# Block-causal attention and FFN: unscaled query split with its subtraction on POOL, single casts, last blocks by DMA, one PSUM bank less per pair

## The chip, the cores and the metric

The kernel runs on one core of a Trainium2 chip. Its engines are TensorE (PE; its weight loads are listed as PEld), VectorE (DVE), ScalarE (ACT), GpSimd (POOL) and SyncE (SP, which only issues DMAs here). Each engine executes its own instructions in order. The metric is the device time of one execution in microseconds, the median over runs.

## The reference

```python
# q, k, v: (8, 8, 576, 64) float32, block = 64
scores = q @ k.T / sqrt(64)
scores = where(row // block >= column // block, scores, -1e9)
attn = exp(scores - max(scores)); attn = attn / (sum(attn) + 1e-9)
x = (attn @ v).transpose(0, 2, 1, 3).reshape(4608, 512)
# w_in (512, 2048), w_out (2048, 512)
h = x @ w_in
g = where(h >= 1, h, where(h <= -1, 0, (h + 1) ** 2 / 4))
out = g @ w_out                      # (4608, 512)
```

## The kernel before

**Numbers.** Matmuls take float32r operands. A float32 value is kept as a sum of two float32r parts, hi (the value cast) and lo (the value less hi), and a product of two such values is made of several matmuls. Queries, keys, values, weights and the FFN's activations are all split so. Attention weights are split too, from the third batch on (the first two are PLAIN and keep theirs in float32).

**Attention** goes over 32 pairs (8 batches by 4 pairs of heads). Each pair is 8 steps of the generator `attention_steps`, whose text sets the order; a scheduler then orders each engine's instructions, and each engine keeps to that order. The names:

- `load` brings q, k and v of the next pair into a pool of three buffers (qn, kn, vn; `nat`). vn takes the buffer that qn had, and it is free once the q subtraction has read it.
- `split_q` and `split_k` make hi and lo side by side (qs, ks), 9 pieces of 64 columns each: 4 tiles for each of two heads and one piece of last blocks. q is multiplied by SCALE = 1/8 in this place. The lo part of q is made on VectorE (L311), that of k on POOL (L321).
- `turned` transposes four 128x128 tiles on TensorE into a bank (ps_qk), ScalarE copies the bank to qb or kb, and SyncE copies half the rows on to qa or ka by DMA. `turned_last` does it with the last block (64 rows) of both heads; there VectorE makes the second copy (L371).
- `scores(j, g)` makes the scores of head j for the query tiles of group g (0, 1, 2), with maxima (L414), exponentials (L418, with the sums), the reciprocal of sum + EPS (L400, L401) and the scaling (L424). `scores_last` does the last 64 query rows of both heads in two halves of 288 columns (L438 to L450).
- The scaled weights pr go through a SyncE DMA into a float32r tile, prr (L246), so that TensorE can transpose them at its float32r rate.
- `turn(j, g)` transposes prr into a bank (ps_t) and `split` makes hi on ScalarE (L454) and lo on VectorE (L456): pa, pb. `turn_last` does this for the last rows; the last key block goes to the tiles pcs (pc), in a bank of its own.
- `attn_v(j)` and `attn_v_first` multiply with the split values (vsr); the last two matmuls of `attn_v` read pcs.

**FFN** is 9 chunks of 512 tokens by 16 columns of w_in. `ffn_in` is 12 matmuls into ph, then the activation (L655 to L661: ACT, DVE, DVE, ACT, POOL); `ffn_out` is 12 matmuls into four output banks. From step 36 of attention on, each step is followed by one FFN step. The weights are converted in 64 pieces (`convert`: ACT, DVE, POOL), in the first 265 us.

**Banks.** PSUM has three banks for all of attention (`work_bank`), one for ph and four for the FFN's output. A bank is taken when the third tile before it has been read. A pair takes 24 of them.

**SyncE's queue** holds all loads and copies in one order, a prr copy behind whatever stands ahead of it. Each of its DMAs also waits for the one that was issued 8 earlier.

Of the kernel before, what the change touches and what calls it, by code (L numbers as in the profile page):

```python
# [8 lines left out]
F32 = mybir.dt.float32  # L9
F32R = mybir.dt.float32r  # L10
AF = mybir.ActivationFunctionType
ALU = mybir.AluOpType
# [11 lines left out]
def block_attn_then_ffn(  # L24
# [226 lines left out]
    class Pair:  # L251
# [52 lines left out]

        def split_q(self):

            qn = self.nat.pop("q")[:, : 2 * NTL + 1, :]
            self.qs = att1.tile([P, 2 * NTL + 1, 2, D], F32R, tag="qs", name="qs")
            for c0, c1 in ((0, 2 * NTL), (2 * NTL, 2 * NTL + 1)):
                nc.vector.tensor_scalar_mul(self.qs[:, c0:c1, 0, :], qn[:, c0:c1, :], SCALE)  # L310
            nc.vector.scalar_tensor_tensor(  # L311
                out=self.qs[:, :, 1, :], in0=qn, scalar=SCALE,
                in1=self.qs[:, :, 0, :].bitcast(F32), op0=ALU.mult, op1=ALU.subtract,
            )

        def split_k(self):
            kn = self.nat.pop("k")[:, : 2 * NTL + 1, :]
            self.ks = att1.tile([P, 2 * NTL + 1, 2, D], F32R, tag="ks", name="ks")
            for c0, c1 in ((0, 2 * NTL), (2 * NTL, 2 * NTL + 1)):
                nc.vector.tensor_copy(self.ks[:, c0:c1, 1, :], kn[:, c0:c1, :])  # L320
            (nc.vector if self.first else nc.gpsimd).tensor_tensor(  # L321
                out=self.ks[:, :, 0, :], in0=kn, in1=self.ks[:, :, 1, :].bitcast(F32),
                op=ALU.subtract,
            )
# [16 lines left out]
        def turned(self, is_q, j):  # L341

            src, a, bt, hi0 = (self.qs, qa, qb, 0) if is_q else (self.ks, ka, kb, D)
            ps = work_bank("ps_qk")
            for t in range(NTL):
                nc.tensor.transpose(  # L346
                    ps[:, t * P : (t + 1) * P].bitcast(F32R), src[:, j * NTL + t, :, :], ident_r
                )

            turned = ps[:, :SM].rearrange("p (t c) -> p c t", t=NTL)  # L350
            nc.scalar.copy(bt[:, j, :SM].rearrange("p (c t) -> p c t", t=NTL), turned)  # L351
            if self.first and j == 0:
                nc.vector.tensor_copy(
                    a[:D, j, :SM].rearrange("p (c t) -> p c t", t=NTL), turned[hi0 : hi0 + D]
                )
            else:
                nc.sync.dma_start(
                    a[:D, j, :SM].bitcast(F32), bt[hi0 : hi0 + D, j, :SM].bitcast(F32)
                )

        def turned_last(self):
# [6 lines left out]
            for i, (a, bt, hi0) in enumerate(((qa, qb, 0), (ka, kb, D))):  # L368
                blocks = ps[:, i * P : (i + 1) * P].rearrange("p (h c) -> p h c", h=2)
                nc.scalar.copy(last_blocks(bt), blocks)  # L370
                nc.vector.tensor_copy(last_blocks(a)[:D], blocks[hi0 : hi0 + D])  # L371
# [55 lines left out]
        def scores_last(self):  # L427
# [14 lines left out]
            nc.vector.tensor_tensor(out=nm[:, 2:3], in0=nm[:, 0:1], in1=nm[:, 1:2], op=ALU.min)  # L442
# [5 lines left out]
            nc.vector.tensor_tensor(out=sm[:, 2:3], in0=sm[:, 0:1], in1=sm[:, 1:2], op=ALU.add)  # L448
            self.inverse(sm[:, 2:3])
# [15 lines left out]
        def turn(self, j, g):  # L465
# [4 lines left out]
            for c0 in range(0, n, P):  # L470
                self.transposed(ps[:, c0 : c0 + P], pr, c0, P)
            if g == 0:
# [8 lines left out]
        def turn_last(self):  # L481
            pr = self.pr.pop("last")
            ps = work_bank("ps_t")
            for c0 in range(0, SM, P):
# [4 lines left out]
            )  # L489
# [82 lines left out]
    def attention_steps():  # L572
# [11 lines left out]
        for i, cur in enumerate(pairs + [None]):  # L584
# [42 lines left out]
            cur.scores(1, 2)  # L627
            cur.attn_v(0)
            cur.turn(1, 0)
# [131 lines left out]
```

## Time and profile before

| | us |
|---|---|
| median of 3 runs | 1270.86 (1270.6 to 1273.3) |
| profiled execution, own time | 1272.09 |
| its span | 1270.3 |

The profile is of one execution. Group rows give line, engine, operation, output <- inputs by the program's names, shapes and count, then busy us, mean ns of one, and the idle time before with what ended it. Timeline rows give start us, length us, engine, line and operation. Idle time of an engine that nobody waits for costs nothing. PE's matmuls overlap in the records: a matmul's start to the next one's start is what the stream takes, not its listed length.

The pairs before FFN steps begin take 22 to 24 us each, the three with the weight conversion beside the FFN about 45 us, and the later ones 33.6 us. The FFN's rest after the last pair begins near 1075 us.

### The profile page before, as it was taken

The page shows a single profiled execution, that of the slowest core. Times are in us where ns is not written, and L with a number is a line of the kernel's source. Part 1 is how long each engine was busy: PE and PEld are TensorE (multiplying, and loading weights), DVE is VectorE, ACT ScalarE, POOL GpSimd, SP SyncE. Part 2 cuts the span into 40 slices and gives each one's busy share as a digit, 9 for nine tenths or more (in the row PEclk, how much of TensorE's full clock was granted, in tenths as well). Part 3 has the DMA queues.
Part 4 walks back from the last instruction along what each step waited for, and adds up shares of the span by engine and source line. Part 5 has one row for each costly group of instructions (what it writes and reads, how often), then busy time and mean ns, then how long its engine had stood idle before and what let it go on. Part 6 is the DMA issues. An engine that isn't in the chain of part 4 may idle for free.

```text
span 1270.3 us, 20591 instructions
## 1 busy us (share of the span) xinstructions
PE 1210.7 (95%) x6496; PEld 1018.4 (80%) x6496; DVE 856.4 (67%) x2164; ACT 701.3 (55%) x1827; POOL 456.3 (36%) x454
## 2 busy tenths in 40 slices
PE   5879887899999999999999999999999999999998
PEld 4667666688888888888888888888888888888886
DVE  8998877857776777777777777777777676222222
ACT  5877656546565655566556656555565564222222
POOL 3555655523332333333333333333333332222222
PEclk9888989899999999999999999999999999999999
DMA  5656666655444545564455545454445443322432
GB/s 157 182 165 213 196 228 210 212 184 173 148 152 147 191 144 161 158 193 149 148 162 168 178 141 161 153 181 143 152 154 184 151 132 117 127 92 97 133 100 100
DMA packets 146093, 201.30 MB, mean 158 GB/s; under 512 B 63152, under 2 KB 93872, under 8 KB 145984
## 3 DMA queue, kind: packets, MB, share of 16 engines
q1 hardware_dynamic: 145984, 199.98, 50.4%
q8 instruction: 52, 0.85, 0.3%
q14 instruction: 57, 0.47, 0.1%
HBM read 120.59 MB, written 17.83 MB: 109 GB/s over the span
## 4 chain that ended last, share of the span: by engine, by line
PE 68%; DVE 8%; ACT 4%; issue 3%; DMA 3%; POOL 2%; SPq 0%; ACTq 0%; POOLq 0%; DVEq 0%
PE ph L646 26%; PE po L670 16%; PE po L675 8%; PE ps_av L500 7%; PE ps_t L461 3%; PE ps_s L394 3%; PE ps_s L391 3%; ACT pr L418 2%; PE ps_qk L346 2%; DMA prr<-pr 2%; DVE t L656 2%; DVE nm L414 1%; DVE t L659 1%; DVE pr L424 1%; POOL work L179 1%
## 5 line engine op out<-in xcount | busy, mean ns | idle before, releaser
L661 POOL TENSOR_TENSOR gl<-t,gh 128x512 fp32r<-128x512 f32 x144 | 186.9, 1298 | 604.7 <-ACT gh L660 301.8
L670 PE MATMUL po<-wo,gh 128*128 128x512 f32 x1152 | 296.9, 399 | 0.1
L656 DVE SCALAR_TENSOR_TENSOR t<-t 128x512 f32<-128x512 f32 x144 | 112.9, 784 | 200.2 <-ACT t L655 198.5
L646 PE MATMUL ph<-xh,wih 128*128 128x512 f32 x576 | 237.6, 413 | 2.7 <-DVE t L659 1.8
L670 PEld LDWEIGHTS po<-wo,gh 128*128 128x128 f32 x1152 | 207.7, 188 | 39.3 <-ACT gh L660 0.6
L646 PE MATMUL ph<-xl,wih 128*128 128x512 f32 x576 | 227.4, 395 | 0.9 <-DVE xl L536 0.9
L646 PE MATMUL ph<-xh,wil 128*128 128x512 f32 x576 | 227.4, 395 | 0.0
L655 ACT ACTIVATE t<-ph 128x512 f32<-128x512 f32 x144 | 86.1, 598 | 184.7 <-PE ph L646 184.7
L418 ACT ACTIVATE pr<-ps_s,nm 128x128 f32<-128x128 f32 (+3 forms) x256 | 134.4, 529 | 50.6 <-DVE nm L414 50.3
L414 DVE TENSOR_REDUCE nm<-ps_s 128x1 f32<-128x128 f32 (+3 forms) x256 | 123.6, 485 | 48.7 <-PE ps_s L394 47.4
L675 PE MATMUL po<-wo,gl 128*128 128x512 f32 x576 | 155.3, 391 | 0.0
L660 ACT CAST gh<-t 128x512 fp32r<-128x512 f32 x144 | 89.6, 622 | 102.1 <-DVE t L659 101.7
L391 PE MATMUL ps_s<-ka,qa 68*128 68x288 f32 (+4 forms) x384 | 122.5, 334 | 9.1 <-ACT kb L351 4.2
L646 PEld LDWEIGHTS ph<-xh,wil 128*128 128x128 f32 x576 | 109.1, 189 | 24.1
L675 PEld LDWEIGHTS po<-wo,gl 128*128 128x128 f32 x576 | 108.1, 188 | 23.3
L646 PEld LDWEIGHTS ph<-xh,wih 128*128 128x128 f32 x576 | 109.1, 189 | 21.7 <-DVE t L659 2.4
L646 PEld LDWEIGHTS ph<-xl,wih 128*128 128x128 f32 x576 | 109.6, 190 | 20.2 <-DVE xl L536 1.5
L394 PE MATMUL ps_s<-kb,qb 128*128 128x288 f32 (+4 forms) x384 | 121.4, 323 | 0.0
L454 ACT CAST pb<-ps_t 128x512 fp32r<-128x512 f32 (+1 forms) x120 | 65.5, 546 | 85.6 <-PE ps_t L461 83.8
L424 DVE TENSOR_SCALAR pr<-pr,sm 128x128 f32<-128x128 f32 (+3 forms) x256 | 104.8, 430 | 4.0
L336 POOL TENSOR_TENSOR vsr<-vn,vsr 64x64 fp32r<-64x64 f32 (+1 forms) x96 | 72.8, 768 | 88.6 <-ACT vsr L335 88.6
L456 DVE TENSOR_TENSOR pb<-ps_t,pb 128x512 fp32r<-128x512 f32 (+1 forms) x120 | 75.6, 630 | 40.4 <-ACT pb L454 39.9
(101 smaller groups left out, 1961.4 us busy)
## 6 DMA issues: line engine op xcount, KB each, us to landing
wo<-wo_split SPq DMA_DIRECT2D x144, 512.0 KB, 3.4
prr<-pr SPq DMA_DIRECT2D x96, 192.0 KB, 2.7
prr<-pr SPq DMA_DIRECT2D x72, 256.0 KB, 2.6
out_dram<-ob SPq DMA_DIRECT2D x36, 256.0 KB, 3.9
qn<-in_q_dram SPq DMA_DIRECT2D x32, 256.0 KB, 2.9
kn<-in_k_dram SPq DMA_DIRECT2D x32, 256.0 KB, 2.9
bits<-in_moe_w_in_dram SPq DMA_DIRECT2D x32, 256.0 KB, 3.6
bits<-in_moe_w_out_dram SPq DMA_DIRECT2D x32, 256.0 KB, 3.2
```

The lines of the kernel that those rows point to most:

```text
L391: nc.tensor.matmul(ps, qa[:KA, j, c0 : c0 + P], ka[:KA, j, k0 : k0 + n], start=first, stop=False)
L394: nc.tensor.matmul(ps, qb[:, j, c0 : c0 + P], kb[:, j, k0 : k0 + n], start=False, stop=last)
L414: nc.vector.tensor_reduce(out=nm[:, i : i + 1], in_=ps[:, cs], axis=AX.X, op=ALU.max, negate=True)
L418: nc.scalar.activation(pr[:, cs], ps[:, cs], AF.Exp, bias=nm[:, i : i + 1], scale=1.0, accum_out=sm[:, i : i + 1],)
L424: nc.vector.tensor_scalar_mul(pr[:, cs], pr[:, cs], sm[:, i : i + 1])
L500: nc.tensor.matmul(ps[:, lo_col:], vt, x, start=first and i == 0 and m == 0, stop=last and i == len(parts) - 1 and m == len(mov) - 1,)
L646: nc.tensor.matmul(ph, w[:, cc, fs], x[:, cc, xs], start=(cc == 0 and i == 0), stop=(cc == NCC - 1 and i == 2),)
L656: nc.vector.scalar_tensor_tensor(out=t_, in0=t_, scalar=1.0, in1=t_, op0=ALU.min, op1=ALU.mult)
L660: nc.scalar.copy(gh, t_)
L661: nc.gpsimd.tensor_tensor(out=gl, in0=t_, in1=gh.bitcast(F32), op=ALU.subtract)
L670: nc.tensor.matmul(po[tt], gh[:, ts_], wo[:, w, :], start=(fc == 0 and w == 0), stop=False)
L675: nc.tensor.matmul(po[tt], gl[:, ts_], wo[:, 0, :], start=False, stop=fc == NFC - 1)
```

## The change

- q is split unscaled, as k is: one cast of 9x64 pieces (before 8 and 1) and one subtraction, and both subtractions are on POOL, except for the first pair. SCALE is multiplied in ScalarE's copy out of the bank instead.
- The second copy of the last blocks (qa, ka) goes by DMA from qb and kb, except for the first pair.
- In `scores_last` the minimum is a scalar operation on one column, and the sum and EPS are added in one instruction.
- The pc transposes share the bank of `turn(1, 0)`, which stands ahead of `attn_v(0)`. A pair takes 23 banks.

```diff
+        def split_qk(self, name, side):
+            x = self.nat.pop(name)[:, : 2 * NTL + 1, :]
+            parts = att1.tile([P, 2 * NTL + 1, 2, D], F32R, tag=name + "s", name=name + "s")
+            hi, lo = parts[:, :, side, :], parts[:, :, 1 - side, :]
+            nc.vector.tensor_copy(hi, x)
+            (nc.vector if self.first else nc.gpsimd).tensor_tensor(
+                out=lo, in0=x, in1=hi.bitcast(F32), op=ALU.subtract
+            )
+            return parts
+
         def split_q(self):
-            qn = self.nat.pop("q")[:, : 2 * NTL + 1, :]
-            self.qs = att1.tile([P, 2 * NTL + 1, 2, D], F32R, tag="qs", name="qs")
-            for c0, c1 in ((0, 2 * NTL), (2 * NTL, 2 * NTL + 1)):
-                nc.vector.tensor_scalar_mul(self.qs[:, c0:c1, 0, :], qn[:, c0:c1, :], SCALE)
-            nc.vector.scalar_tensor_tensor(
-                out=self.qs[:, :, 1, :], in0=qn, scalar=SCALE,
-                in1=self.qs[:, :, 0, :].bitcast(F32), op0=ALU.mult, op1=ALU.subtract,
-            )
+            self.qs = self.split_qk("q", 0)
...
-            nc.scalar.copy(bt[:, j, :SM].rearrange("p (c t) -> p c t", t=NTL), turned)
+            scale = SCALE if is_q else 1.0
+            nc.scalar.mul(bt[:, j, :SM].rearrange("p (c t) -> p c t", t=NTL), turned, scale)
...
-                nc.scalar.copy(last_blocks(bt), blocks)
-                nc.vector.tensor_copy(last_blocks(a)[:D], blocks[hi0 : hi0 + D])
+                nc.scalar.mul(last_blocks(bt), blocks, 1.0 if i else SCALE)
+                if self.first:
...
+                else:
+                    nc.sync.dma_start(
+                        last_blocks(a)[:D].bitcast(F32), last_blocks(bt)[hi0 : hi0 + D].bitcast(F32)
+                    )
...
-            nc.vector.tensor_tensor(out=nm[:, 2:3], in0=nm[:, 0:1], in1=nm[:, 1:2], op=ALU.min)
+            nc.vector.tensor_scalar(
+                out=nm[:, 2:3], in0=nm[:, 0:1], scalar1=nm[:, 1:2], scalar2=None, op0=ALU.min
+            )
...
-            nc.vector.tensor_tensor(out=sm[:, 2:3], in0=sm[:, 0:1], in1=sm[:, 1:2], op=ALU.add)
-            self.inverse(sm[:, 2:3])
+            nc.vector.tensor_scalar(
+                out=sm[:, 2:3], in0=sm[:, 0:1], scalar1=sm[:, 1:2], scalar2=EPS,
+                op0=ALU.add, op1=ALU.add,
+            )
+            nc.vector.reciprocal(sm[:, 2:3], sm[:, 2:3])
...
         def turn(self, j, g):
             for c0 in range(0, n, P):
                 self.transposed(ps[:, c0 : c0 + P], pr, c0, P)
+            if j == 1 and g == 0:
+                ps_c = ps[:BLK, n : n + P]
+                self.transposed(ps_c, self.pr.pop("last"), SM, BLK)
+                self.split(
+                    ps_c.rearrange("p (h c) -> p h c", h=2), *(x[:BLK] for x in self.pc)
+                )
...
         def turn_last(self):
-            ps = work_bank("ps_t")
-            self.transposed(ps[:BLK, :P], pr, SM, BLK)
-            self.split(
-                ps[:BLK, :P].rearrange("p (h c) -> p h c", h=2), *(x[:BLK] for x in self.pc)
-            )
...
             cur.scores(1, 2)
+            cur.turn(1, 0)
             cur.attn_v(0)
-            cur.turn(1, 0)
```

Three places show how the instructions stand on an engine, always in a pair of the later part (33.6 us each). A row gives the line, the operation and the output's shape. The numbers behind a tile's name are buffer numbers.

First TensorE, after the scores(1,1) matmuls (L394 writes the last of them). ps_t are transposes of weights, ph is `ffn_in`, ps_qk the transposes of the next pair's keys. Before:

```order
L394 MATMUL ps_s<-kb,qb 128x384
L461 MATMUL ps_t<-ident_r,prr 128x128 x4
L461 MATMUL ps_t<-ident_r,prr 64x128
L646 MATMUL ph<-xh,wih 128x512
L646 MATMUL ph<-xl,wih 128x512
L646 MATMUL ph<-xh,wil 128x512
L646 MATMUL ph<-xh,wih 128x512
L646 MATMUL ph<-xl,wih 128x512
L646 MATMUL ph<-xh,wil 128x512
L346 MATMUL ps_qk<-ident_r,ks 128x128 x4
```

After:

```order
L398 MATMUL ps_s<-kb,qb 128x384
L470 MATMUL ps_t<-ident_r,prr 128x128 x4
L342 MATMUL ps_qk<-ident_r,ks 128x128 x4
L657 MATMUL ph<-xh,wih 128x512
L657 MATMUL ph<-xl,wih 128x512
L657 MATMUL ph<-xh,wil 128x512
```

The key transposes have moved ahead of the twelve `ffn_in` matmuls, and the 64x128 transpose of the pc block has left this place.

TensorE again, from scores(1,2) to `ffn_out` (L670 before, L681 after). Before:

```order
L394 MATMUL ps_s<-kb,qb 128x512
L500 MATMUL ps_av<-pb_7956,vsr_109 128x320
L500 MATMUL ps_av<-pb_7957,vsr_109 128x320
...
L500 MATMUL ps_av<-pcs_107,vsr_109 128x64
L500 MATMUL ps_av<-pcs_108,vsr_109 128x64
L461 MATMUL ps_t<-ident_r,prr 128x128 x3
L670 MATMUL po<-wo,gh 128x512 x8
```

After:

```order
L398 MATMUL ps_s<-kb,qb 128x512
L470 MATMUL ps_t<-ident_r,prr 128x128 x3
L470 MATMUL ps_t<-ident_r,prr 64x128
L511 MATMUL ps_av<-pb_7878,vsr_109 128x320
L511 MATMUL ps_av<-pb_7879,vsr_109 128x320
...
L511 MATMUL ps_av<-pcs_107,vsr_109 128x64
L511 MATMUL ps_av<-pcs_108,vsr_109 128x64
L681 MATMUL po<-wo,gh 128x512 x8
```

The transposes of turn(1,0), with the pc block's as the last of them, stand ahead of attn_v(0), which reads that block in its last two matmuls.

SyncE's queue, at the start of a pair: copies of weights (prr), of last blocks (L373), loads of v, q and k. Before:

```order
L246 DMA prr<-pr 128x384
L285 DMA vn<-in_v_dram 128x4x64
L246 DMA prr<-pr 128x384
L285 DMA vn<-in_v_dram 128x4x64
L289 DMA vn<-in_v_dram 64x2x64
L295 DMA qn<-in_q_dram 128x2x256
L300 DMA qn<-in_q_dram 64x64 x2
L295 DMA kn<-in_k_dram 128x2x256
L300 DMA kn<-in_k_dram 64x64
L246 DMA prr<-pr 128x512
```

After:

```order
L246 DMA prr<-pr 128x384
L373 DMA qa<-qb 64x2x64
L246 DMA prr<-pr 128x384
L373 DMA ka<-kb 64x2x64
L285 DMA vn<-in_v_dram 128x4x64 x2
L289 DMA vn<-in_v_dram 64x2x64
L295 DMA qn<-in_q_dram 128x2x256
L300 DMA qn<-in_q_dram 64x64 x2
L295 DMA kn<-in_k_dram 128x2x256
L300 DMA kn<-in_k_dram 64x64
L246 DMA prr<-pr 128x512
```

Between the second and the third prr copy stand 9 issues where there were 7: one last block and the first load of v have come in.

More of the change, by code (lines that the diff above doesn't have):

```diff
@@ L303, in load @@
             self.nat[name] = t_
[L305 to L324 removed]
+        def split_qk(self, name, side):
[7 more added lines that the diff above has]
+            return parts
+        def split_q(self):
+            self.qs = self.split_qk("q", 0)
+        def split_k(self):
+            self.ks = self.split_qk("k", 1)
         def split_v(self):
@@ L369, in turned_last @@
                 blocks = ps[:, i * P : (i + 1) * P].rearrange("p (h c) -> p h c", h=2)
[L370 to L371 removed]
+                nc.scalar.mul(last_blocks(bt), blocks, 1.0 if i else SCALE)
+                if self.first:
+                    nc.vector.tensor_scalar_mul(
+                        last_blocks(a)[:D], blocks[hi0 : hi0 + D], 1.0 if i else SCALE
+                    )
[3 more added lines that the diff above has]
+                    )
         def begin_a(self):
@@ L481, in turn_last @@
         def turn_last(self):
-            pr = self.pr.pop("last")
+            pr = self.pr["last"]
             ps = work_bank("ps_t")
```

6 lines of the change are left out of this document (3 added, 3 removed).

## The prediction

> **What bounds the kernel now.** I read the page's totals first, then busy time by stretch, then the instructions of one pair in order of time. Stretch rows give start:end, length, and the busy time of PE, PEld, DVE, ACT and POOL with counts, then the granted clock, the DMA share and GB/s. The second table counts the q subtraction (L311) alone, which is one per pair.
>
> ```profile
> span 1270.3 us, 20591 instructions
> PE 1210.7 (95%) x6496; PEld 1018.4 (80%) x6496; DVE 856.4 (67%) x2164; ACT 701.3 (55%) x1827; POOL 456.3 (36%) x454
> ...
> 25.00:113.00 88.00, 71.97 (x386) 58.24 (x386) 80.40 (x247) 69.57 (x214) 47.61 (x60) 0.88 0.62 184
> 113.00:268.00 155.00, 136.76 (x667) 107.95 (x668) 119.12 (x290) 97.44 (x274) 85.99 (x102) 0.95 0.67 212
> 268.00:1075.00 807.00, 799.35 (x4551) 685.47 (x4550) 584.08 (x1488) 474.81 (x1229) 269.03 (x242) 1.00 0.51 158
> 1075.00:1270.30 195.30, 190.19 (x841) 156.61 (x839) 52.72 (x78) 46.50 (x79) 45.38 (x35) 1.00 0.32 108
> ...
> 25.00:113.00 88.00, 2.95 (x4) 0.88 0.62 184
> 113.00:268.00 155.00, 2.23 (x3) 0.95 0.67 212
> 268.00:1075.00 807.00, 16.87 (x23) 1.00 0.51 158
> ```
>
> There are four regimes. From 25 to 113 us VectorE is busy 80.40 of 88 us (91%) and sets the pace. From 113 to 268 us no engine is full (DVE 77%, PE 88%). From 268 to 1075 us TensorE is busy 799.35 of 807 us; with 23 subtractions there and the last pair's, I count 24 pairs, 33.6 us each. There only what makes PE itself stand still, or keeps its stream from flowing, counts. After 1075 us no attention is left and the change touches nothing.
>
> **Front, 25 to 113 us: VectorE's instructions.** Group rows below: busy us, then mean ns of one, then idle time before. Rows with x32 are of the whole run, the others of 20 to 265 us.
>
> ```profile
> L311 DVE SCALAR_TENSOR_TENSOR qs<-qn,qs 128x576 fp32r<-128x576 f32 x8 | 6.5, 808 | 0.0
> L310 DVE TENSOR_SCALAR qs<-qn 128x512 fp32r<-128x512 f32 x7 | 3.4, 482 | 0.0
> L310 DVE TENSOR_SCALAR qs<-qn 128x64 fp32r<-128x64 f32 x8 | 2.4, 297 | 0.0
> L320 DVE CAST ks<-kn 128x512 fp32r<-128x512 f32 x8 | 3.5, 442 | 0.0
> L320 DVE CAST ks<-kn 128x64 fp32r<-128x64 f32 x8 | 2.5, 314 | 1.7 <-DMA kn<-in_k_dram 1.7
> L442 DVE TENSOR_TENSOR nm<-nm 128x1 f32<-128x1 f32 x8 | 2.1, 268 | 0.0
> L448 DVE TENSOR_TENSOR sm<-sm 128x1 f32<-128x1 f32 x8 | 2.1, 261 | 3.0 <-ACT pr L444 3.0
> L371 DVE CAST ka<-ps_qk 64x128 fp32r<-64x128 f32 x7 | 2.0, 293 | 0.5 <-ACT kb L370 0.4
> L371 DVE CAST qa<-ps_qk 64x128 fp32r<-64x128 f32 x7 | 1.9, 271 | 0.0
> L400 DVE TENSOR_SCALAR sm<-sm 128x1 f32<-128x1 f32 x38 | 5.5, 144 | 2.4 <-ACT pr L418 2.1
> L450 DVE TENSOR_SCALAR pr<-pr,sm 128x576 f32<-128x576 f32 x32 | 17.6, 549 | 0.9
> ...
> 24.15 1.40 POOL L321 TENSOR_TENSOR ks<-kn,ks 128x576 fp32r<-128x576 f32 x1 [0.85 <-DVE ks L320]
> 24.60 1.11 DVE L167 TENSOR_SCALAR work<-work 128x256 f32<-128x256 f32 x1
> ...
> 229.64 0.28 DVE L167 TENSOR_SCALAR work<-work 128x256 f32<-128x256 f32 x1
> ```
>
> Removed from VectorE per pair: the q subtraction, 0.81 us; the two last-block copies, 0.27 + 0.29; and of the small operations L442, L448 and one L400 (0.27 + 0.26 + 0.14), in whose place two one-column scalar operations at 0.14 stand: 0.38. Together 1.75 us.
>
> The casts: 0.48 + 0.30 for q and 0.44 + 0.31 for k, 1.53 in all, become two of 128x576. No row shows a cast of 576 into pieces 64 wide. The bounds are 0.55 (L450, one source, contiguous on both sides) and 0.81 (L311, two sources into the same pieces), so a gain of 0.43 or a loss of 0.09. I take 0.77, no change, nearest L311 because the destination's pattern is the same.
>
> Added: POOL's second subtraction blocks VectorE. The L167 that started inside POOL's k subtraction took 1.11 us, and outside it 0.28: 0.83 lost. The bounds are 0 (nothing of that kind issued meanwhile) and 1.40 (the whole subtraction); I take 1.0, near the row, with a little for a second operation hit. Net, 1.75 - 1.0 = 0.75 us less per pair. Over 4 pairs, at the 91% to which VectorE sets the pace, this is -2.7 us.
>
> [...]
>
> ACT's copies become scaled copies of the same tiles on the same engine; I cost them at 0. The first pair's lines stay on VectorE.
>
> **Middle, 113 to 268 us.** The chain of waits from 150 to 260 us, by line:
>
> ```profile
> by line: issue 20.1%; POOL work L179 12.4%; DMA bits<-in_moe_w_in_dram 8.0%; PE ps_av L500 6.0%; PE ph L646 4.5%; POOL wil L183 4.5%; DVE work L170 4.4%; DVE work L167 3.4%; ACT work L165 3.4%; POOL ws L183 3.1%; POOL gl L661 2.7%; DVE work
> ```
>
> POOL has 12.4 + 4.5 + 3.1 + 2.7 = 22.7% of it. Added are 3 subtractions of 1.40 us, of which 22.7% lie on the chain: +0.9. Removed are 0.75 us by 3 pairs on VectorE, at a half, my choice since it is not full: -1.1. Net -0.2. Ends: +4.2 if POOL's added time lies on the chain whole, -2.2 if VectorE's does.
>
> **Steady pairs, 268 to 1075 us.** First the bank. These are TensorE and ScalarE in one pair, start and length, then one group row of TensorE over the run (idle before the group and its releaser).
>
> ```profile
> 661.37 0.58 ACT L418 ACTIVATE pr<-ps_s,nm 128x384 f32<-128x384 f32 x1 [0.37 <-DVE nm L414]
> 661.48 0.39 PE L646 MATMUL ph<-xh,wil 128*128 128x512 f32 x1
> 662.10 0.54 PE L346 MATMUL ps_qk<-ident_r,ks 128*128 128x128 f32 x4 [0.23 <-ACT pr L418]
> 662.47 0.47 PE L646 MATMUL ph<-xh,wih 128*128 128x512 f32 x1
> ...
> L346 PE MATMUL ps_qk<-ident_r,ks 128*128 128x128 f32 x256 | 33.1, 255 | 4.3 <-ACT pr L418 3.8 <-ACT pc L454 0.2
> ```
>
> The k transposes wait for a work bank that the exponential of scores(1,1) still reads. The matmul before starts at 661.48, they at 662.10: 0.62, where undisturbed matmuls of 0.39 follow each other by 0.24 (eight in 2.08, in the third table below). That is 0.38 lost, of which 0.23 is listed as idle. The run lists 3.8 us of such idle time, or 16.5 such stalls, 0.26 us per pair over 24. In the new order the k transposes follow turn_last's at once, and without the pc bank theirs is the bank of the q transposes, long copied out: the stall goes. The 12 ffn_in matmuls also run unbroken; the break costs 0.08 (the first after it took 0.47, one in the stream 0.39). Together -0.34 per pair. Ends: 0 if the earlier transposes wait for something else, -0.46 if every pair stalled.
>
> Second, SyncE's queue and the third float32r copy of weights (prr of scores(0,2)). Rows: two issues of one pair and the transposes that want the third copy, the same of a pair where it was late, and the landing time (last number).
>
> ```profile
> 647.86 0.49 SPq L246 DMA_DIRECT2D prr<-pr  x1
> 652.76 0.54 SPq L246 DMA_DIRECT2D prr<-pr  x1
> 656.06 0.47 PE L461 MATMUL ps_t<-ident_r,prr 128*128 128x128 f32 x4
> ...
> 754.31 0.54 SPq L246 DMA_DIRECT2D prr<-pr  x1
> 757.24 0.52 PE L461 MATMUL ps_t<-ident_r,prr 128*128 128x128 f32 x4 [0.43 <-DMA prr<-pr]
> ...
> prr<-pr SPq DMA_DIRECT2D x72, 256.0 KB, 2.6
> ```
>
> From the second copy (647.86) to the third (652.76) there are 7 issues, so 8 steps of 0.61 us. The change puts ka's last block and one v load among them: 1.2 us more, issue at 653.98, landing 2.6 later at 656.58, while PE asks at 656.06: a wait of 0.5. The v load goes later because its buffer is freed by the q subtraction, now on POOL. In the pair with the late issue PE waited 0.43, and its transposes start 2.93 after the issue (754.31 to 757.24), where the other pair had 3.30. The lower bound is 0, since the issues need not keep 0.61; I take the middle, +0.25. Queued behind on SyncE are only weight loads and copies wanted later. The last blocks themselves, 62 issues, are read only by scores_last, a step later: 0.
>
> Third, the pc blocks. Their transposes join turn(1,0), now just ahead of attn_v(0), whose last matmuls want them.
>
> ```profile
> 664.60 0.69 DVE L414 TENSOR_REDUCE nm<-ps_s 128x1 f32<-128x512 f32 x1 [1.57 <-PE ps_s L394]
> 665.20 0.68 DVE L656 SCALAR_TENSOR_TENSOR t<-t 128x512 f32<-128x512 f32 x1
> 665.48 0.33 PE L500 MATMUL ps_av<-pcs,vsr 128*128 128x64 f32 x2
> 665.64 0.45 PE L461 MATMUL ps_t<-ident_r,prr 128*128 128x128 f32 x3
> 665.92 2.08 PE L670 MATMUL po<-wo,gh 128*128 128x512 f32 x8
> ```
>
> Three transposes took 0.28 (665.64 to 665.92), four about 0.37, so PE reaches the pc matmuls at 665.85, and the second of them, which needs the subtraction, about 0.1 later. VectorE, by its new order, first ends the reduction and L656 at 665.88, then the subtraction, some 0.28 as the small operations above: 666.16. PE waits 0.2; bounds 0 and 0.31. POOL's added 1.40 us per pair I cost at 0 here: it is busy 269 of 807 us.
>
> **The sum.** -0.34 + 0.25 + 0.2 = +0.11 per pair, by 24: +2.6. With -2.7 and -0.2: -0.3 us on the profiled execution, whose own time is 1272.1 (the span and 1.8 around it), 1.2 above the median 1270.86. On the median: 1270.6, no change that a measurement could tell; its resolution is 0.2%, 2.5 us.
>
> **Rivals.** (1) Faster: neither new wait comes, because the issues move up and the pc blocks are ready. For it: the undisturbed pair's copy lands 0.7 ahead of its use (3.30 less 2.6); against it, the pair with the late copy. -0.34 by 24 = -8.2, -2.9 in front: 1259.8, and with fast casts (0.43 by 4 by 0.91, -1.6) 1258.2. (2) Slower: the train on SyncE alone costs what its rows say, 0.5 us per pair, the rest as above: -0.34 + 0.2 + 0.5 = +0.36 by 24 = 8.6, less 2.9: 1276.6. It decides from 0.37 us per pair up (0.23 net by 24, less 2.9, is 2.6 us); the late pair's 0.43 speaks for it, the other pair's slack of 0.7 against. (3) The lock: POOL's added time stays on the middle's chain whole, +3.3 more, and takes 1.40 per pair in front, +1.5 more: 1275.4. (4) The change does not do what it says: other waits fill the bank's place and the removed operations were all covered; 1271.
>
> **Chances.** Forecast 0.42 (of it faster 0.12, same 0.20, slower 0.10; its own range, by the ends of single terms, 1265 to 1276), rival 1 0.27 (all faster), rival 2 0.17 and rival 3 0.06 (slower), rival 4 0.08 (same). So faster 0.39, same 0.28, slower 0.33. The range goes from rival 1 with fast casts, 1258.2, to rival 2 with the front's gain of 2.9 lost, 1279.5.
>
> **What the new profile would show.** Right: k transposes right behind turn_last with no wait on ACT; the transposes of scores(0,2) waiting some 0.25 us on the DMA of prr; a wait of 0.2 ahead of the last pc matmul; casts of 576 near 0.77 us; VectorE's operations beside POOL's 31 new subtractions lengthened; VectorE under 91% in the front. Wrong: if these transposes start without a wait, the time is nearer 1260; if a scores matmul waits for ka or qa, the last blocks' transfer was not free.

## The result and the profile after

The changed kernel takes 1318.08 us (1316.64 to 1325.56) where the kernel before took 1271.41 in the same comparison: a ratio of 1.0377, interval 1.0336 to 1.0418. That is 3.8% slower and outside the range, on the side of rivals 2 and 3, at a larger price than either had. The page and the stretches of the changed kernel, columns as before:

```profile
span 1314.9 us, 20771 instructions
...
PE 1223.0 (93%) x6496; PEld 1023.6 (78%) x6496; DVE 834.9 (63%) x1975; ACT 699.2 (53%) x1827; POOL 476.4 (36%) x485
...
25.00:113.00 88.00, 70.98 (x378) 56.47 (x379) 78.54 (x214) 66.89 (x204) 47.89 (x61) 0.90 0.55 159
113.00:268.00 155.00, 128.70 (x602) 101.37 (x602) 112.38 (x263) 92.56 (x258) 84.57 (x102) 0.88 0.65 208
```

VectorE's busy time fell by 21.5 us (856.4 to 834.9), as it was meant to, and the span grew by 44.6. From 113 to 268 us PE did 8 us less work than before in the same stretch (128.70 against 136.76). Fixed stretches do not hold the same work, so I split the spans at the start of each pair, which is its first transpose in `turned_last`:

| us | before | after | difference | forecast |
|---|---|---|---|---|
| up to pair 0 | 9.6 | 10.2 | +0.6 | 0 |
| pairs 0 to 3 (front) | 91.5 | 88.9 | -2.6 | -2.7 |
| pairs 4 to 7 (middle) | 167.6 | 183.4 | +15.8 | -0.2 |
| pairs 8 to 30 (steady, 23) | 778.9 | 811.0 | +32.1 | +2.5 |
| rest, to the start of the last matmul | 217.2 | 215.9 | -1.3 | +0.1 |

In the steady pairs the loss is at the transposes of weights. These are TensorE's waits from 268 to 1130 us: what it waited for, us in total, times, longest. First before, then after.

```profile
PE ps_t L461 <- DMA prr<-pr: 3.2, 5, 1.6
PE ps_qk L346 <- ACT pr L418: 2.9, 13, 0.3
```

```profile
PE ps_t L470 <- DMA prr<-pr: 22.1, 26, 2.9
```

The wait for the bank is gone, as forecast, and the wait for prr copies has grown sevenfold. One pair of the changed kernel shows how: SyncE's queue from the second to the third copy, then TensorE.

```profile
563.37 0.22 PE L362 MATMUL ps_qk<-ident_r,qs 128*128 128x128 f32 x1
...
567.34 0.49 SPq L246 DMA_DIRECT2D prr<-pr  x1
567.92 0.62 SPq L373 DMA_DIRECT2D ka<-kb  x1
568.63 1.10 SPq L285 DMA_DIRECT2D vn<-in_v_dram  x2
569.78 0.65 SPq L289 DMA_DIRECT2D vn<-in_v_dram  x1
570.53 0.55 SPq L295 DMA_DIRECT2D qn<-in_q_dram  x1
571.12 2.32 SPq L300 DMA_DIRECT2D qn<-in_q_dram  x2
573.54 0.53 SPq L295 DMA_DIRECT2D kn<-in_k_dram  x1
574.12 0.48 SPq L300 DMA_DIRECT2D kn<-in_k_dram  x1
574.72 0.52 SPq L246 DMA_DIRECT2D prr<-pr  x1
...
575.60 0.28 PE L398 MATMUL ps_s<-kb,qb 128*128 128x256 f32 x1
578.79 0.50 PE L470 MATMUL ps_t<-ident_r,prr 128*128 128x128 f32 x4 [2.91 <-DMA prr<-pr]
...
579.47 2.80 PE L681 MATMUL po<-wo,gh 128*128 128x512 f32 x6
```

This pair has the longest wait of all. The copy is issued 11.35 us after the pair's start (the median pair's at 10.44). It stands behind nine other issues, of which one took over a microsecond longer than its like, and TensorE stands still for 2.91 us. The six matmuls in the last row then take 2.80 us where eight took 2.08 in the kernel before. TensorE's granted clock, the third number from the right in these rows of TensorE alone, is down after the stop:

```profile
571.00:575.60 4.60, 4.60 (x29) 1.00 0.53 122
578.79:582.50 3.71, 3.71 (x16) 0.60 0.26 67
```

Two signs of the prediction are in the rows that follow: the k transposes stand right behind turn_last with no wait, and the casts and POOL's new subtraction (group rows of 20 to 265 us, and of the run) cost 0.74 and 1.43 us, where I had taken 0.77 and 1.40.

```profile
511.01 0.46 PE L470 MATMUL ps_t<-ident_r,prr 128*128 128x128 f32 x4
511.31 0.50 PE L342 MATMUL ps_qk<-ident_r,ks 128*128 128x128 f32 x4
511.65 0.46 PE L657 MATMUL ph<-xh,wih 128*128 128x512 f32 x1
...
L310 DVE CAST qs<-qn 128x576 fp32r<-128x576 f32 x8 | 5.9, 743 | 0.0
L311 POOL TENSOR_TENSOR qs<-qn,qs 128x576 fp32r<-128x576 f32 x31 | 44.4, 1432 | 49.8 <-DVE qs L310 47.9 <-DVE sm L404 1.8
```

### The profile page after: what moved, and what is told of

Read it like the earlier page. It is cut to its first block, busy times and chain, and to the rows that moved or that the text cites. A ratio compares the mean times of both kernels' runs of the same rounds, so it can differ in the third digit from the quotient of the medians.

```text
span 1314.9 us, 20771 instructions
## 1 busy us (share of the span) xinstructions
PE 1223.0 (93%) x6496; PEld 1023.6 (78%) x6496; DVE 834.9 (63%) x1975; ACT 699.2 (53%) x1827; POOL 476.4 (36%) x485
## 5 line engine op out<-in xcount | busy, mean ns | idle before, releaser
L672 POOL TENSOR_TENSOR gl<-t,gh 128x512 fp32r<-128x512 f32 x144 | 190.2, 1321 | 619.8 <-ACT gh L671 390.1
L681 PE MATMUL po<-wo,gh 128*128 128x512 f32 x1152 | 303.9, 405 | 0.7 <-DMA wo<-wo_split 0.6
L681 PEld LDWEIGHTS po<-wo,gh 128*128 128x128 f32 x1152 | 211.5, 191 | 41.3 <-DMA wo<-wo_split 1.0
L667 DVE SCALAR_TENSOR_TENSOR t<-t 128x512 f32<-128x512 f32 x144 | 104.5, 726 | 208.5 <-ACT t L666 207.1
L657 PEld LDWEIGHTS ph<-xh,wil 128*128 128x128 f32 x576 | 108.9, 189 | 24.5
L428 DVE TENSOR_SCALAR pr<-pr,sm 128x128 f32<-128x128 f32 (+3 forms) x256 | 116.4, 475 | 5.8 <-DVE sm L405 0.3
L470 PEld LDWEIGHTS ps_t<-ident_r,prr 128*128 128x128 f32 x600 | 64.7, 139 | 51.3 <-issue 17.3
```

The source lines that it names most:

```text
L428: nc.vector.tensor_scalar_mul(pr[:, cs], pr[:, cs], sm[:, i : i + 1])
L657: nc.tensor.matmul(ph, w[:, cc, fs], x[:, cc, xs], start=(cc == 0 and i == 0), stop=(cc == NCC - 1 and i == 2),)
L667: nc.vector.scalar_tensor_tensor(out=t_, in0=t_, scalar=1.0, in1=t_, op0=ALU.min, op1=ALU.mult)
L672: nc.gpsimd.tensor_tensor(out=gl, in0=t_, in1=gh.bitcast(F32), op=ALU.subtract)
L681: nc.tensor.matmul(po[tt], gh[:, ts_], wo[:, w, :], start=(fc == 0 and w == 0), stop=False)
```

## The experiments

Two theories for the steady pairs were set against each other. Q: the third copy is late because of its place in SyncE's queue. T: the small transfers of the last blocks, or POOL's work, slow things in another way. For all runs "steady" is the mean of pairs 8 to 30, and "early" the time from pair 0's start to pair 8's: 33.87 and 259.1 us before, 35.26 and 272.3 after. "Excess" at a place is the time from one matmul's start to the next, less an allowance of mine for its columns, summed over those 23 pairs. The allowance is the same in every run, and a little under what the trace before shows from one start to the next without a wait (0.12 us in the median for 256 columns, 0.23 for 512).

**Parts undone, or done alone (e1 to e4).**

```diff
 # e1: the changed kernel, last blocks by VectorE
-                if self.first:
+                if True:
                     nc.vector.tensor_scalar_mul(
                         last_blocks(a)[:D], blocks[hi0 : hi0 + D], 1.0 if i else SCALE
 # e2: e1, and the q subtraction on VectorE
-            (nc.vector if self.first else nc.gpsimd).tensor_tensor(
+            (nc.vector if self.first or name == "q" else nc.gpsimd).tensor_tensor(
 # e3: the kernel before, with the change of turn, turn_last and the order of turn(1, 0) alone
 # e4: the kernel before, last blocks by DMA
+                if self.first:
                     nc.vector.tensor_copy(last_blocks(a)[:D], blocks[hi0 : hi0 + D])
+                else:
+                    nc.sync.dma_start(
+                        last_blocks(a)[:D].bitcast(F32), last_blocks(bt)[hi0 : hi0 + D].bitcast(F32)
+                    )
```

> The changed kernel with the last blocks copied by VectorE again. Its SyncE queue then has a v load back in front of the second prr copy, but the scheduler puts 9 issues between the second and the third prr copy all the same (a k block and a weight load come in). Theory Q (place in the queue: each issue ahead of the third copy delays it by 0.6 us): TensorE waits about as long at these transposes as in the changed kernel, 1.0 to 1.3 us per pair, and the time stays at 1310 to 1320 us. Rival T (the last blocks' small transfers themselves slow the queue or the other transfers): the wait goes, 24 times 1.1 less, about 1290 us.

Measured: 1363.78 us, ratio 1.0747 (1.0719 to 1.0776); steady 37.64, early 264.5. Without the last blocks' DMA the steady pairs became slower still, so those transfers are not the cause that T takes them for (POOL's subtraction stays in e1), but Q had the size wrong too. One pair:

```profile
574.62 0.22 PE L362 MATMUL ps_qk<-ident_r,qs 128*128 128x128 f32 x1
...
585.62 0.54 SPq L674 DMA_DIRECT2D wo<-wo_split  x1
586.25 1.78 SPq L246 DMA_DIRECT2D prr<-pr  x3
...
586.85 0.28 PE L398 MATMUL ps_s<-kb,qb 128*128 128x256 f32 x1
590.41 0.72 PE L470 MATMUL ps_t<-ident_r,prr 128*128 128x128 f32 x4 [3.29 <-DMA prr<-pr]
...
591.44 3.74 PE L681 MATMUL po<-wo,gh 128*128 128x512 f32 x8
```

The scheduler put the 512 KB weight load ahead of the copy. The copy was issued 11.63 us into the pair and landed 4.0 us later, not 2.8. To this comes the clock. The next rows are the stretches before and after the stop, with TensorE's busy time, the granted clock, DMA share and GB/s:

```profile
583.00:586.80 3.80, 3.80 (x23) 1.00 0.48 130
590.41:593.61 3.20, 3.19 (x13) 0.50 0.06 15
593.61:596.81 3.20, 3.20 (x10) 0.60 0.12 28
```

After 3.29 us of standing still the clock is at 0.50, then 0.60 in the mean, for 6.4 us. Between the `ffn_out` matmuls alone the steady pairs have 22.5 us of excess more than before.

> The changed kernel with the last blocks copied by VectorE and the q subtraction on VectorE again; left of the change are the bank, the single casts, the unscaled split and the small operations. 8 issues stand between the second and third prr copy (7 before the change, 9 with it). Theory Q: a wait of 0.3 to 0.6 us per pair at these transposes, the bank's 0.3 gained back, and the stretch from 100 to 270 us as before the change if the q subtraction on POOL caused its loss of 16 us: 1270 to 1278 us. Rival B (the bank and the new order of turn(1,0) cause the middle's loss): 1285 to 1292 us.

Measured: 1318.08 us, 1.0386 (1.0366 to 1.0407); steady 35.64, early 264.4. Both expectations missed on the steady pairs: +12.3 us at the third copy, as Q had it, but +12.3 also between the matmuls of scores_last (waits for a bank that an exponential still reads), and 5.5 after turn_last. The queue is not all that moves: undoing an edit gives the scheduler another order on every engine.

> The kernel before with the pc bank's change alone (pc transposes in turn(1,0)'s bank, turn(1,0) ahead of attn_v(0)). 7 issues between the second and third prr copy, as before. Theory Q: the stall ahead of the k transposes goes, 0.3 us per pair by 24, little comes for the pc blocks (0.05 per pair): 1263 to 1267 us. Rival B (the reordering makes new waits in the middle): 1275 to 1287 us.

Measured: 1271.32 us, 1.0012 (0.9998 to 1.0026): no difference, and between the two expectations. In the steady pairs both parts are there: -5.9 us of excess ahead of the k transposes, and +4.3 (the weights of turn(1,0), wanted sooner) and +3.3 (the pc blocks).

```profile
PE ps_t L461 <- DMA prr<-pr: 4.6, 11, 1.2
```

> The kernel before with the last blocks by DMA alone. 8 issues between the second and third prr copy. Theory Q: 0.3 to 0.6 us per pair at the transposes of scores(0,2), by 24, less 2 us in front: 1276 to 1284 us. Rival T (the transfers themselves): the whole 1.16 us per pair, 1295 to 1300 us. Rival P (only POOL's subtraction matters): no change, 1269 to 1272 us.

Measured: 1310.12 us, 1.0328 (1.0296 to 1.036); steady 35.24, early 272.7. All three expectations were too low. The last blocks' DMA alone brings most of the loss: +21.1 us of excess at the third copy and +13.6 before pair 8. The wait per pair (1.02) was twice what Q gave for 8 issues: in e4's order the weights themselves were scaled later, 10.5 us into the pair (8.8 before), which took the copy's slack, and the 0.8 us that it then stood in the queue counted in full.

**The order of the queue set by hand (e5 to e12).** In each the loads of q and k of the next pair are made to stand behind a given prr copy, on the changed kernel (e5, e9), the kernel before (e6, e10), e2 (e7), e1 (e11) and e3 (e8, e12).

```diff
 # e5 to e8: behind scores_last's copies of this pair; e9 to e12: behind those of the pair before
-                nxt.load("q")
-                nxt.load("k")
+                with tc.issue_after(copy.ins):
+                    nxt.load("q")
+                    nxt.load("k")
```

> The changed kernel with one thing added, and nothing left out: from the third batch on, the loads of the next q and k stand in SyncE's queue behind the copies of scores_last's weights instead of among the prr copies. Between the second and the third prr copy stand then a last block and a weight load (2 issues, not 9). Theory Q (the place of the third copy in the queue is the loss of the steady pairs): the wait of 1.16 us per pair ahead of the transposes of scores(0,2) falls under 0.15, steady pairs at 33.5 to 34.2 us, the time 1286 to 1296 us; the loss before 280 us stays. Rival T (the 62 small transfers or POOL's added work slow the steady pairs in another way): the wait only moves to other transposes, 1310 to 1320 us.

Measured: 1347.98 us, 1.0611 (1.056 to 1.0662); steady 36.78. TensorE's waits:

```profile
PE ps_qk L343 <- POOL qs L312: 38.0, 22, 2.6
PE ps_t L471 <- DMA prr<-pr: 4.3, 4, 1.8
```

The excess at the third copy fell from 26.8 to 1.1 us, as Q said, and a new wait of 44.6 came ahead of the q transposes, so the time is over both expectations. I had misread the queue: the loads that stand among the copies are those of the pair after next, so my edge made each a whole pair late.

> The kernel before with the same order of loads alone. Theory Q: the third copy had slack there already (wait 0.1 us per pair), so the gain is that wait and the few late pairs, 1 to 4 us: 1266 to 1270 us. Rival L (the loads, moved later, come late for their casts): 1275 us or more.

Measured: 1303.96 us, 1.0261 (1.0228 to 1.0295). Rival L, for the same reason: +27.4 us ahead of the q transposes.

> The changed kernel with last blocks and q subtraction on VectorE, and the same order of loads. Theory Q: of its 35.6 us per steady pair the 0.53 of the third copy's transposes goes, 12 us; the waits of scores_last on a bank (0.5 per pair) stay if they come from VectorE's casts in a row: 1302 to 1308 us. Rival C (these waits too come from late copies and loads): both go, 1288 to 1296 us.

Measured: 1323.65 us, 1.0418 (1.0384 to 1.0452); steady 35.90. Neither expectation; +23.0 us stand ahead of the q transposes here too.

> The kernel before with the pc bank's change and the same order of loads. Theory Q: the bank's gain of 0.26 us per pair is kept, the waits it made at turn(1,0) (0.2 per pair) shrink if the copies come earlier: 1260 to 1268 us. Rival: they come from the transposes' new place and stay, 1268 to 1272 us.

Measured: 1319.63 us, 1.0386 (1.0346 to 1.0427). The same miss.

> The changed kernel, nothing left out, with the loads of q and k behind the weight copies of the pair before: the loads that stand among the prr copies are those of a pair further on, so the run before this one had put them 33 us too late, and TensorE waited for the q subtraction instead. Now 5 issues stand between the second and the third prr copy (9 in the changed kernel). Theory Q: the wait of 1.16 us per pair at the transposes of scores(0,2) falls under 0.2, and no wait for the q subtraction comes: steady pairs 33.9 to 34.3 us, 1286 to 1296 us. Rival T (any queue order makes a wait of the kind): over 1310 us.

Measured: 1302.27 us, 1.0256 (1.0232 to 1.028); steady 34.63. The excess at the third copy fell from 26.8 to 5.6 us, and no wait for q came, but 18.4 us stand at the transposes of turn(1,0) (8.2 in the changed kernel), whose copy now has loads of q and k and a weight load just ahead of it. So 14.6 of the 32.1 us came back, and the time lies between the two expectations.

> The kernel before with the loads of q and k behind the weight copies of the pair before. Theory Q: it had no wait there to lose but the late pairs (0.1 us each): 1267 to 1272 us. Rival: the loads now stand among the copies of qa and ka and delay those: 1275 us or more.

Measured: 1286.37 us, 1.0122 (1.0107 to 1.0137). The rival's time, but not its path: +10.5 us stand at the transposes of turn(1,1) and +3.5 at those of turn(1,0), and what TensorE waits for is prr copies (13.2 us), not qa or ka.

> The changed kernel with the last blocks copied by VectorE again and this order of loads. Theory Q: of 37.6 us per steady pair the wait of 2.4 and the slow clock after it (about 1 us) go, 33.9 to 34.2 remain; before 275 us it is as the run with the last blocks on VectorE: 1272 to 1282 us.

Measured: 1293.28 us, 1.0181 (1.0151 to 1.0212); steady 34.77, 2.87 us a pair less than e1, with the slow clock gone (excess between the `ffn_out` matmuls 18.4, from 39.9). Most of what is left of the loss is 22.2 us at turn(1,0), and the expected 1272 to 1282 us was not reached.

> The kernel before with the pc bank's change and this order of loads. Theory Q: 33.6 to 33.8 us per steady pair, the bank's gain kept and a part of the wait at turn(1,0) gone: 1263 to 1270 us. Rival: the wait at turn(1,0) is the scaling's latency and stays, 1270 to 1273 us.

Measured: 1313.19 us, 1.034 (1.0294 to 1.0387): 36.9 us at turn(1,0), where the transposes ask sooner and the copy comes later. Both expectations missed.

**Loads off the queue, and the middle (e13 to e16).**

```diff
 # e13 (the changed kernel), e14 (the kernel before): loads of q, k, v from the third batch on
-                nc.sync.dma_start(
+                (nc.sync if self.plain else nc.scalar).dma_start(
 # e15: the changed kernel, last blocks' DMA issued by ScalarE
-                    nc.sync.dma_start(
+                    nc.scalar.dma_start(
                         last_blocks(a)[:D].bitcast(F32), last_blocks(bt)[hi0 : hi0 + D].bitcast(F32)
 # e16: the changed kernel, q subtraction on VectorE (as in e2)
```

> The changed kernel with the loads of q, k and v from the third batch on issued by ScalarE instead of SyncE; nothing is left out. Theory Q (the steady loss is the place of the prr copies among the loads on one queue): no prr copy is behind a load any more, and the waits of TensorE for them (26.8 + 4 + 3.6 us in the changed kernel) fall under 6: steady pairs 33.6 to 34.1 us, 1283 to 1292 us, the loss before 280 us stays. Rival A (each issue holds ScalarE for half a microsecond and its exponentials come late): new waits of TensorE on ScalarE, 1300 us or more.

Measured: 1322.34 us, 1.0415 (1.0383 to 1.0446); steady 35.51. The excess at the third copy is 27.6 us, as in the changed kernel. TensorE itself hardly waits for ScalarE, but rival A's path is there one step earlier. ScalarE stands still for 41.4 us in 21 of the pairs until the q subtraction on POOL ends, since the load of v that it is to issue needs the buffer that this subtraction reads (the load goes out 0.03 us behind it). Its exponentials of scores(0,2) start 0.84 us later than in the changed kernel, and the weights are scaled 10.01 us into the pair, not 8.35. The copy then goes out at once.

> The kernel before with the same loads issued by ScalarE. Theory Q: little was lost to the queue before, so 1264 to 1271 us; rival A: 1275 us or more.

Measured: 1290.20 us, 1.016 (1.0127 to 1.0193); steady 34.64. Its time is rival A's, but ScalarE is not late here (the weights are scaled at 8.71 us). These two bring Q down in its simple form: no load of q, k or v stands ahead of the copy on SyncE, the copy goes out as soon as its weights are scaled, and yet it is late. A pair of e14:

```profile
588.53 0.33 SPq L663 DMA_DIRECT2D wo<-wo_split  x1
589.41 5.05 SPq L246 DMA_DIRECT2D prr<-pr  x3
...
592.80 0.28 PE L394 MATMUL ps_s<-kb,qb 128*128 128x256 f32 x1
593.99 0.51 PE L461 MATMUL ps_t<-ident_r,prr 128*128 128x128 f32 x4 [0.91 <-DMA prr<-pr]
```

The copy is issued early, 8.8 us after the pair's start, right behind a weight load, while ScalarE's queue brings q and k. It landed 4.4 us after its issue, where the same copy took 2.8 in the kernel before. What made it longer no run here shows by itself, since in e14 the weight load stands just ahead too, and in e1 that alone went with 4.0.

> The changed kernel with the last blocks' 62 copies still by DMA but issued by ScalarE, which has just written them. One issue fewer stands between the second and third prr copy (8). Theory Q: the wait there falls from 1.16 to 0.4 to 0.8 us per pair, and the 8 us that the last blocks' DMA costs before 280 us go, if they are SyncE's head-of-line waits: 1292 to 1304 us. Rival D (there it is the 2.2 us until the copy lands that delays scores_last): before 280 us as the changed kernel, 1302 to 1312 us.

Measured: 1366.99 us, 1.0755 (1.0727 to 1.0783); steady 37.58, early 267.5. The scheduler's order is e1's again, weight load ahead of the copy, with the same price. So neither expectation held. Early, 4.8 of the 13 us came back.

> The changed kernel with the q subtraction on VectorE again, the last blocks still by DMA. 8 issues stand between the second and third prr copy, but both last blocks are ahead of the second. Theory Q: a wait of 0.6 to 1.0 us per pair there. If POOL's queue caused the loss from 100 to 280 us (TensorE waits 9.7 us there for subtractions on POOL), 8 us go and the time is 1298 to 1308 us; if the last blocks' DMA did, it stays at 1308 to 1318 us.

Measured: 1307.49 us, 1.0294 (1.0272 to 1.0315); steady 35.18, early 265.5. That is within the range for POOL. In the early part 6.8 us came back, and the wait at the third copy was 1.08.

From here the theory is of the copy's arrival, issue plus landing. Medians over 22 steady pairs (9 to 30), from the records of the queue, all in us after the pair's start but for landing and wait. "Scaled" is the end of VectorE's scaling of scores(0,2), before which the copy can't go. "Arrival" is the sum of the medians of issue and landing. "Asked" is the time at which the transposes would start if they waited for nothing: the start of the scores matmul ahead of them, plus the allowance for its columns.

| kernel | scaled | issue | landing | arrival | asked | mean wait |
|---|---|---|---|---|---|---|
| before | 8.80 | 9.07 | 2.81 | 11.87 | 12.32 | 0.09 |
| after | 8.35 | 10.44 | 2.82 | 13.26 | 12.33 | 1.20 |
| e16 | 10.18 | 10.60 | 2.68 | 13.28 | 12.75 | 1.08 |
| e4 | 10.50 | 10.92 | 2.80 | 13.72 | 13.09 | 1.04 |
| e13 | 10.01 | 10.04 | 3.84 | 13.88 | 12.78 | 1.24 |
| e14 | 8.71 | 8.74 | 4.43 | 13.17 | 12.33 | 1.01 |
| e1 | 8.60 | 10.69 | 3.98 | 14.67 | 12.33 | 2.54 |
| e15 | 8.35 | 10.45 | 3.97 | 14.42 | 12.32 | 2.45 |
| e9 | 8.35 | 8.39 | 3.90 | 12.29 | 12.32 | 0.24 |
| e17 | 8.35 | 8.37 | 2.34 | 10.71 | 12.33 | 0.02 |

Where the arrival lies behind the asking the wait is there, and is the difference plus 0.1 to 0.6; where it lies 0.4 or more ahead there is next to none; e9 is level and waits 0.24. The column "scaled" shows what held the copy: in the changed kernel, e1 and e15 it stood 2.1 us in the queue with its weights ready, in e13 and e14 not at all, and in e4 and e16 the weights were late themselves, so that the 0.8 to 0.9 us in the queue found no slack.

**The copy put ahead of everything (e17, e18).** On the changed kernel and on e3, the loads of q and k behind the third copy of the pair before, and the weight load of that step behind the third copy.

```diff
+        gate, copied["gate"] = copied["gate"], None     # the third copy, once
+        if gate:
+            with tc.issue_after(gate.ins):
+                nc.sync.dma_start(wo.bitcast(F32), wo_split[fc])
```

> The changed kernel, nothing left out, with the third prr copy directly behind the v loads (4 issues behind the second copy, not 9), the weight load of that step behind it, and the loads of q and k behind both. Arrival theory (TensorE waits at the transposes of scores(0,2) for the copy's arrival, that is its issue plus its landing time, which is 2.8 us, and about 4 when a 512 KB weight load was issued just ahead): issue near 8.4 us after the pair's start, arrival near 11.2, before TensorE wants it at 12.3; the 1.1 us per pair go and no other copy is later than in the changed kernel: steady pairs 33.7 to 34.1 us, 1284 to 1292 us, with the 13 us before 280 us left. If other waits come in its place once more: over 1298 us.

Measured: 1299.00 us, 1.0225 (1.0202 to 1.0248); steady 34.48, early 273.8. The copy came at 10.71 us, as expected, and TensorE no longer waited for it (excess 26.8 to 0.4). But the steady pairs are 0.4 us over the expectation: the loads pushed back, and a weight load, now stand just ahead of the copy for turn(1,0). They hardly delay its issue (0.17 us behind the scaling in the mean), but it takes 3.69 us to land, 2.88 in e3, and with the third copy's wait gone it is asked for 1.4 us sooner than in the changed kernel. TensorE's waits, and that place in one pair (start 562.07), where the copy took 4.06 us to land:

```profile
PE ps_t L471 <- DMA prr<-pr: 17.6, 21, 2.1
...
579.66 0.41 SPq L688 DMA_DIRECT2D wo<-wo_split  x1
580.17 0.50 SPq L247 DMA_DIRECT2D prr<-pr  x1
...
581.97 0.40 PE L399 MATMUL ps_s<-kb,qb 128*128 128x512 f32 x1
582.21 1.76 PE L695 MATMUL po<-wo,gh 128*128 128x512 f32 x7
584.27 0.52 PE L471 MATMUL ps_t<-ident_r,prr 128*128 128x128 f32 x4 [0.30 <-DMA prr<-pr]
```

> The kernel before with the pc bank's change and the same order of copies and loads; a version that could beat both. Arrival theory: 33.4 to 33.7 us per steady pair (the bank's stall is gone, the copies of turn(1,0) a little earlier): 1262 to 1268 us. If the wait at turn(1,0) is the scaling's own latency, 1268 to 1272 us, as the kernel before.

Measured: 1304.87 us, 1.0255 (1.0231 to 1.028). Third copy in time (wait 0.02), but 32.2 us of excess at turn(1,0) (7.4 in e3), whose copy arrives at 21.9 us, 20.4 in e3. So the version that was to beat both kernels does not, and nor does any other here; e3 is level with the kernel before.

## Why the prediction was wrong

**The failed step is the second term of the steady pairs**, "the lower bound is 0, since the issues need not keep 0.61; I take the middle, +0.25". It measured 24.5 us over 23 pairs, 1.07 each, four times the term and twice its upper end of 0.5. The mechanism was right (rival 2 names it), and three numbers in it were off. The issue moved by 1.37 us (9.07 to 10.44), not 1.2. Landing and slack were both taken from rows that did not belong together: the median over all 72 copies of 2.6, and one pair's slack of 0.7; for this copy landing is 2.81 and the slack 0.45. And there was no ground for the middle: the pair with the late issue, which was in my rows, had waited 0.43 for 9.99, and the new issue was to come later than that. With the row's own numbers, 1.37 less 0.45 is 0.9, and 0.1 to 0.6 pass between landing and start.

The mean hides two kinds of pair. In 12 of the table's 22 no issue ahead of the copy took over 0.8 us; the copy went out at 10.2 us in the median and the wait was 0.68 in the mean, not far from rival 2's 0.5. In the other 10 one issue took 0.9 to 2.1 us, and the wait was 1.80: 18 of the 26 us. The kernel before has 5 such pairs, and they cost it 0.17 each, because its slack took them up. The prediction had one of them in its rows and priced none. What makes an issue slow no run shows.

That the queue's order is the cause is shown by the changed kernel, e9 and e17 together. In all three the weights are ready at 8.35 us; e9 and e17 change by hand only the order of SyncE's queue, the copy goes out 2.1 us sooner, and the wait goes with it. An estimate from the records says the same: had the changed kernel's copy gone out when its weights were scaled, and landed as long after as it did, one of the 22 pairs would have waited for it, for 0.1 us.

**Left out** was that the reorder takes the slack from turn(1,0)'s copy. In e3 its transposes ask for it at 20.24 us, in the kernel before at 21.83, and it arrives near 20.4 in both. In the changed kernel copy and asking are both later and still level (21.5). Excess at these transposes rose from 3.1 us to 8.2 (e3: 7.4). The prediction costed turn(1,0)'s move only through the pc blocks.

**Right:** the bank. -5.9 us, 0.26 a pair, as worked out; e3 shows it alone. The pc blocks cost something, +1.9 us of excess ahead of the second pc matmul (0.08 a pair, not 0.2). The sizes of the casts and of the subtraction on POOL were right: 743 and 1432 ns against 770 and 1400. The casts' 743 ns lie nearer the bound of 0.81 us than that of 0.55. ScalarE's scaled copies took 602 ns where the plain ones took 590.

**Right in number alone:** the front, -2.6 against -2.7. e3, which changes nothing on VectorE, has -3.2 in the same four pairs, and its pairs 4 to 7 take 3.3 us longer. So the number does not show that VectorE's removed operations were worth it.

**The middle, -0.2 forecast, +15.8 measured.** The steps that failed are the last blocks' DMAs, which had no price there, and "22.7% lie on the chain" for POOL's subtractions. Kernels that differ only in later pairs repeat the early time well: 269.9 to 273.8 us for the changed kernel's early part (e5, e9, e13, e17), 259.1 to 260.3 for that of the kernel before (e6, e10, e14). Against this:

| early part, us | |
|---|---|
| before; e3 (bank alone) | 259.1; 259.2 |
| e4 (before + last blocks by DMA) | 272.7 |
| after | 272.3 |
| after without the last blocks' DMA (e1) | 264.5 |
| after without the q subtraction on POOL (e16) | 265.5 |
| after without both (e2) | 264.4 |

So the last blocks' DMA costs 13.6 us alone, 7.8 in the changed kernel; the subtraction on POOL costs 6.8 with that DMA and nothing without; and 5 us remain with the casts, the scaling and the small operations. From 99 to 283 us TensorE waits 7.1 us for subtractions on POOL, which the kernel before did not have among its longest. But e16, with the q subtraction on VectorE, waits 7.3 us at the same transposes, so these waits are not what the move to POOL costs. First the changed kernel, then e16:

```profile
PE ps_qk L342 <- POOL qs L311: 4.7, 2, 2.8
PE ps_qk L342 <- POOL ks L311: 2.4, 2, 1.9
...
PE ps_qk L342 <- DVE qs L311: 5.1, 3, 2.3
PE ps_qk L342 <- POOL ks L311: 2.2, 2, 1.6
```

The parts do not add up, and every variant orders the conversion differently. Which single wait carries the rest stays open. e15 moved the DMA off SyncE's queue and got back 4.8 of 7.8 us, which points to that queue without settling it.

Rival 1 had its chance of 0.27 on "the undisturbed pair's copy lands 0.7 ahead of its use". That slack was one pair's; the median is 0.45.

## What to carry to other kernels

When one queue carries both latency-bound copies and prefetches, cost an added issue by the arrival of the first copy behind it. That is the later of two times, when its data is ready and when the queue reaches it, plus the landing time of that very copy. Set it against the time at which it is wanted, pair by pair: the slack is the small difference of these, it must not come from an average over other copies, and it also has to take up the occasional slow issue. A prefetch pushed back doesn't vanish, it comes next to another copy: with the order set by hand, the changed kernel got 19 of its 47 us back at best (e17), and without the last blocks' DMA (e11) it still ended 22 us above the kernel before. And where a scheduler orders the queues, undoing half of a change is a new order everywhere, so a part's cost is read from the excess at its place, not from the total, and a number that comes out right may belong to another part (the front).

## What the runs showed of the hardware

- The third copy of a pair, 256 KB from SBUF to SBUF, landed 2.3 to 2.8 us after its issue in the median (before, after, e4, e16, e17), and 3.8 to 4.4 in e1, e9, e13, e14 and e15, where a 512 KB weight load had been issued 0.4 to 2.1 us ahead. e13 and e14 have loads on ScalarE's queue as well; no run has those without the weight load.
- After two stops in the changed kernel's steady pairs TensorE's granted clock was 0.50 for 3.4 us (from 579.56 and from 965.27 us), and in e1's pair above it was 0.50 for 3.2 us, then 0.60 in the mean for another 3.2. In e1's steady pairs 19 of the 21 stops over 0.9 us were followed by it, from 1.67 us up, but of the changed kernel's 12 only those of 1.80 and 2.91 us, and not one of 2.56. Between the `ffn_out` matmuls alone e1 has 22.5 us of excess more than the kernel before, and e15 25.9.
